# Queries, keys and third weights of a fused attention and two-layer MoE kernel: 154 transposes from fp32 to fp32r, with a new written-out order

## The chip, the cores and the metric

The kernel runs on one core of a Trainium2 chip. The metric is the device time of one execution in microseconds (us); three runs of the kernel before gave a median of 740.92 us (740.73 to 741.88). Five engines work from queues of their own, each strictly in its order: TensorE (PE, with its weight loads shown apart as PEld), VectorE (DVE), ScalarE (ACT), GpSimd (POOL), and SyncE (SP), which here only issues DMAs.

## The reference

For 2 batches of 8 heads, each of 768 positions by 64, queries and keys are assigned to one of 16 clusters (the largest product of the normalized row with normalized centroids). Attention is taken within a cluster: pairs of unequal assignment are masked out. Its output (1536 tokens by 512) goes through two dense layers in sequence.

```python
q_assign = np.argmax(np.einsum('bhsd,hcd->bhsc', q_n, c_n), axis=-1)
k_assign = np.argmax(np.einsum('bhsd,hcd->bhsc', k_n, c_n), axis=-1)
mask = q_assign[:, :, :, None] == k_assign[:, :, None, :]
scores = np.where(mask, scale * np.matmul(q, k.transpose(0, 1, 3, 2)), -1000000000.0)
attn = softmax(scores)
x = np.matmul(attn, v)                   # heads joined: 1536 x 512
h = (x @ w1) * (x @ w2) @ w3 @ w_out     # first layer
g = h2 * clip(h2 + 3, 0, 6) / 6          # with h2 = h @ w_in of the second layer
out = g @ w_out2
```

## The kernel before

Everything on PE is computed to nearly fp32 precision with fp32r operands: each operand is split into a high part (an ACT copy rounded to fp32r) and a low part (the rest, a subtraction), and a product takes three matrix multiplications (high by high, high by low, low by high), or two where operands are stacked.

The work has these stages. **Attention** (to about 350 us) goes head by head: load q and k of a head side by side into one tile of 128 partitions by 6 blocks of 128 columns (`load_qk`, L582 to L585), transpose it by PE in two groups of three (`qk_T`, L605 to L608), take high parts on ACT (`qk_hi`) and low parts on DVE (`qk_lo`), move halves by DMA, compute assignments (`assign_mm` on PE, then nine small steps `oh0` to `oh8`, L651 to L677, on DVE and partly POOL, of which the last transposes the codes, `cd`), and copy the codes into the key and query tiles (`codes_C`). The scores of six blocks c follow (`scores`, L737, a large part and a small part, which waits for the exponential before), then the row maximum on DVE (`smax`, L758), the exponential on ACT (`sexp`, L780), transposes of the exponentials on PE (`p_T`, L796), high and low parts and the product with v (`av`, L820).

**Weights** are brought in meanwhile: each block of 128 by 512 passes through `conv_ops` (two ACT copies, a clamp L1008 on POOL or DVE, two bit operations on DVE, L1017 and L1021). The blocks of w3 are then transposed on PE, four 128 by 128 pieces at a time (`w3_T`, L1037 to L1040), split, and multiplied by w_out (`w_mm`, L1068), so that the first layer's last two matrices become one. Then come the products with w1 and w2 (L1144; from 198 us on beside attention), the combined matrix (L1259 and L1396, to about 485 us) and the second layer (L1707 and L1751) to the end. From the combined matrix on the kernel uses sums of blocks in place of some products, and those sums are DVE's work.

**The order** is written out by hand in a table, `RANK`: each operation of each kind has its place in one sequence of some 4000, and each engine issues its operations in that sequence. A second table, `ON`, says for operations that could run on several engines which one takes it (d, a, p for DVE, ACT, POOL). Room in tile rings is counted when the table is read. `idle_pe` (L529 to L534) puts in 21 multiplications without use, in the first 35 us.

An exponential tile is already transposed as fp32r: `p_raw` (L763 to L772) declares a second tile of type fp32r over the same memory, and writes one padding column of it, so that the transposes have a writer to wait for:

```python
t = at.tile([128, 3 * S + 8], F32R, tag=f"p{hf}", name="praw")
pad = t[:, 3 * S:3 * S + 1]
w = (nc.gpsimd if e == "pool" else nc.vector).tensor_copy(out=pad, in_=three)
...
x = nc.tensor.transpose(pt[:, blk(j)], raw[h, hf][0][:, c, blk(kb)], id_r)
tc.add_manual_dep(x.ins, raw[h, hf][1].ins.name, SYNC)
```

Queries, keys and w3 are transposed as fp32, with the fp32 identity `id_f`.

Of the kernel before, what the change touches and what calls it, by code (L numbers as in the profile page):

```python
# [8 lines left out]
F32 = mybir.dt.float32  # L9
# [73 lines left out]
    "S1": """  # L83
# [3 lines left out]
        1912 1937 1949 1970 1984 2009 2029 2045 2058 2067 2096""",  # L87
    "S": """
# [3 lines left out]
        1892 1925 1940 1960 1979 1994 2015 2034 2049 2069 2088 2101""",  # L92
    "mx": """
# [3 lines left out]
        1899 1928 1944 1968 1982 2000 2019 2038 2053 2073 2090 2107""",  # L97
    "ex": """
# [278 lines left out]
def cluster_attention_moe_kernel(  # L377
# [57 lines left out]
    def blk(i):  # L435
        return slice(i * 128, i * 128 + 128)
# [1422 lines left out]
```

## Time and profile before

| | |
|---|---|
| median of three runs | 740.92 us (740.73 to 741.88) |
| the profiled execution | 741.47 us, its span 739.7 us |
| PE busy | 719.0 us (97%), 4143 instructions |
| PE weight loads busy | 661.4 us (89%) |
| DVE busy | 611.5 us (83%), 1060 instructions |
| ACT busy | 546.8 us (74%), 1043 instructions |
| POOL busy | 201.9 us (27%), 258 instructions |
| DMA moved | 101.97 MB, mean 138 GB/s |

The profile is of one execution. Busy time is what an engine spent in instructions; a matrix multiplication is pipelined, so that the next starts before it ends, and its duration is longer than the step from one to the next. How long an engine needs for one is read from starts. The span runs from the first to the last instruction; the execution's own time lies 1.8 us around it.

### The profile page before, as it was taken

How to read it: one execution, taken by the hardware profiler on the slowest of the kernel's cores; microseconds unless marked ns; L12 is line 12 of the kernel's file. 1: busy time of each engine (PE TensorE's matmuls, PEld its weight loads, DVE VectorE, ACT ScalarE, POOL GpSimd, SP SyncE). 2: the span in 40 equal slices, each digit the busy share in tenths (PEclk: the TensorE clock that was granted, in tenths of full speed). 3: DMA queues.
4: the chain of work that ended last, by engine and by line, in shares of the span. 5: the costliest groups of instructions: out<-in, count | busy, mean ns of one | idle time of the engine just before them, and what ended most of it. 6: DMA issues, size and time to landing. Idle time of an engine off the chain costs nothing. (4 is left out here: it accounts for less than half of the span.)

```text
span 739.7 us, 12102 instructions
## 1 busy us (share of the span) xinstructions
PE 719.0 (97%) x4143; PEld 661.4 (89%) x4143; DVE 611.5 (83%) x1060; ACT 546.8 (74%) x1043; POOL 201.9 (27%) x258
## 2 busy tenths in 40 slices
PE   5699999999999999999999999999999999999998
PEld 4488888888999999999999999999888998998986
DVE  6999999999899888778999999888897666666542
ACT  4899999898888878789867676676666656564543
POOL 3452646332635263355301110110110210011100
PEclk9999999999999999999999999999999999999999
DMA  8668555465563656453566752633222221411202
GB/s 237 157 167 221 152 150 162 114 161 140 150 185 119 182 155 170 115 156 114 178 200 228 238 175 100 220 122 138 91 86 85 72 72 60 137 61 58 72 28 86
DMA packets 81742, 101.97 MB, mean 138 GB/s; under 512 B 30960, under 2 KB 56592, under 8 KB 81680
## 3 DMA queue, kind: packets, MB, share of 16 engines
q1 hardware_dynamic: 81680, 101.20, 45.7%
q8 instruction: 33, 0.54, 0.3%
q14 instruction: 29, 0.24, 0.1%
HBM read 71.34 MB, written 15.78 MB: 118 GB/s over the span
## 5 line engine op out<-in xcount | busy, mean ns | idle before, releaser
L424 DVE TENSOR_TENSOR pl<-ptr,ph 128x512 fp32r<-128x512 f32 x144 | 96.3, 681 | 7.3 <-ACT ph L427 6.9
L758 DVE TENSOR_REDUCE den<-pst 128x1 f32<-128x768 f32 x96 | 91.1, 949 | 10.3 <-PE pst L746 9.2
L427 ACT ACTIVATE ph<-ptr 128x512 fp32r<-128x512 f32 x144 | 84.4, 597 | 14.0 <-PE ptr L796 9.7
L780 ACT ACTIVATE p<-pst,den 128x768 f32<-128x768 f32 x96 | 86.8, 904 | 8.8 <-DVE den L758 7.5
L1144 PE MATMUL psab<-xT,abhl 128*128 128x384 f32 x384 | 81.2, 343 | 0.6 <-DVE g L1154 0.6
L1008 POOL TENSOR_SCALAR cvt<-cvt 128x512 f32<-128x512 f32 x55 | 39.3, 718 | 142.0 <-ACT cvt L427 110.3
L746 PE MATMUL pst<-kk,qkL 128*128 128x512 f32 (+1 forms) x192 | 71.4, 374 | 4.8 <-ACT p L780 4.7
L1144 PEld LDWEIGHTS psab<-xT,abhl 128*128 128x128 f32 x384 | 65.4, 188 | 2.0 <-DVE g L1154 0.9
L820 PE MATMUL av<-ph,vs 128*128 128x384 f32 x192 | 66.4, 346 | 0.0
L796 PEld LDWEIGHTS ptr<-id_r,praw 128*128 128x128 f32 x576 | 60.9, 140 | 5.8 <-DVE pl L424 0.2
L746 PE MATMUL pst<-kk,qkH 128*128 128x512 f32 (+1 forms) x192 | 64.2, 338 | 1.7 <-ACT qkH L427 1.3
L820 PE MATMUL av<-pl,vs 128*128 128x384 f32 x192 | 64.8, 338 | 0.0
L427 ACT ACTIVATE m_sn<-psh 128x384 f32<-128x384 f32 x64 | 31.3, 489 | 44.3 <-PE psh L1707 43.4
L796 PE MATMUL ptr<-id_r,praw 128*128 128x128 f32 x576 | 63.6, 240 | 0.0
L427 ACT ACTIVATE cvt<-raw 128x512 f32<-128x512 f32 x72 | 48.1, 672 | 11.8 <-DVE cvs L1021 6.8
L1017 DVE SCALAR_TENSOR_TENSOR cvs<-cvt,cvs 128x512 int32<-128x512 int32 x72 | 50.0, 696 | 7.5 <-POOL cvt L1008 4.2
L1021 DVE SCALAR_TENSOR_TENSOR cvs<-cvt,cvs 128x512 int32<-128x512 int32 x72 | 50.8, 709 | 0.4
L427 ACT ACTIVATE cvs<-raw 128x512 int32<-128x512 uint8 x72 | 48.1, 670 | 1.8 <-DMA set<-cvs 1.8
L1068 PE MATMUL psw<-woh,wT 128*128 128x512 f32 x128 | 49.3, 405 | 0.0
L746 PEld LDWEIGHTS pst<-kk,qkL 128*128 128x128 f32 x192 | 36.0, 187 | 12.2 <-ACT p L780 9.9
L1751 PE MATMUL po<-m_whl,m_gv 128*128 128x512 f32 x162 | 44.0, 393 | 0.0
L1729 ACT ACTIVATE tt<-m_sn,three 128x384 f32<-128x384 f32 x48 | 29.4, 613 | 18.8 <-DVE m_sn L1717 9.0
(198 smaller groups left out, 1836.0 us busy)
## 6 DMA issues: line engine op xcount, KB each, us to landing
raw<-in_moe_w_dram SPq DMA_DIRECT2D x32, 512.0 KB, 4.3
m_gb<-set SPq DMA_DIRECT2D x64, 256.0 KB, 2.9
raw<-in_moe_w_out_dram SPq DMA_DIRECT2D x24, 512.0 KB, 3.4
raw<-in_moe_w_in_dram SPq DMA_DIRECT2D x16, 512.0 KB, 4.9
set<-cvs SPq DMA_DIRECT2D x32, 256.0 KB, 3.0
kk<-qkH SPq DMA_DIRECT2D x16, 384.0 KB, 4.0
abp<-cvs SPq DMA_DIRECT2D x16, 256.0 KB, 2.8
b_gv<-abp SPq DMA_DIRECT2D x16, 256.0 KB, 4.7
```

The costliest lines, as they stand in the source:

```text
L424: nc.vector.tensor_tensor(out=out, in0=a, in1=b, op=ALU.subtract)
L427: nc.scalar.activation(out=out, in_=in_, func=AF.Copy, **kw)
L746: x = mm(out=psr[:, t, ks_], lhsT=TT[nm, h][:, i, cs_], rhs=flat(TT["K", h][:, a])[:, ks_], start=st, stop=sp)
L758: done["mx", n] = [other_banks(nc.vector.tensor_reduce(out=den_at(h, 0, c), in_=psS[h, c], axis=AX.X, op=ALU.max, negate=True), ("S", n + 1))]
L780: done["ex", n] = [other_banks(nc.scalar.activation(out=p, in_=psS.pop((h, c)), func=AF.Exp, bias=den_at(h, 0, c), accum_out=den_at(h, 1, ...
L796: x = nc.tensor.transpose(pt[:, blk(j)], raw[h, hf][0][:, c, blk(kb)], id_r)
L820: mm(out=t[:, 0:HF], lhsT=vs_t[h][:, 2 * s + i, :], rhs=x_[:, c0:c0 + HF], start=(s == 0 and i == 0 and n == 0), stop=(s == 2 and i == 1 a ...
L1017: stt(out=s, in0=cvt[key], scalar=3, in1=s, op0=ALU.logical_shift_left, op1=ALU.bitwise_or)
L1021: stt(out=s, in0=cvt.pop(key), scalar=-0x80000000, in1=s, op0=ALU.bitwise_and, op1=ALU.bitwise_or)
L1068: mm(out=ps, lhsT=wT[m, hf][:, a, blk(kk)], rhs=w_[hf][:, kk, :], start=(kk == 0 and n == 0), stop=(kk == 3 and n == 2))
L1144: mm(out=ps[:, 0:HF], lhsT=s[:, w, a, blk(kk)], rhs=xT0[0][:, x_, kk, hf * HF:hf * HF + HF], start=(kk == 0 and n == 0), stop=(kk == KD - ...
L1751: mm(out=outs[b, c], lhsT=g[:, a, blk(c % 3)], rhs=w[:, w_, :], start=(first and a == 0 and w_ == 0), stop=(last and a == 1))
```

## The change

Queries and keys of heads 1 to 15 and all blocks of w3 are transposed as fp32r, from a second tile over the same memory, with the fp32r identity `id_r`. For each tile there is a new operation that writes one padding column: `tw` (15 times) and `ww` (16 times), on an engine that `ON` names. Head 0 stays fp32. So that the second tile has the same place as the first, the rings of two and three buffers (`qkn`, `cvs`) become tiles named one by one. The table of places is new throughout, and so is `ON`: seven more clamps stand on DVE (24 for 17), and five more of the one-hot steps `oh1` and `oh4` (8 for 3). The first table lines, and the core of the code:

```diff
-    "lq": "0 1 62 156 297 185 446 611 849 970 1052 1221 1163 1322 1545 1618",
-    "lk": "5 8 96 191 345 403 496 754 886 999 1115 1260 1185 1368 1567 1752",
+    "lq": "0 5 66 131 164 380 458 577 724 900 975 1194 1220 1357 1502 1641",
+    "lk": "4 7 71 212 374 423 466 609 824 956 1008 1208 1380 1462 1611 1676",
...
+    "tw": "ddpappppaaaapaa",
+    "ww": "dpadaadpppaadppp",
...
+    def pad_write(e, pad):
+        if e == "act":
+            return nc.scalar.activation(out=pad, in_=three, func=AF.Copy)
+        return (nc.gpsimd if e == "pool" else nc.vector).tensor_copy(out=pad, in_=three)
...
+    def qk_raw(e, h):
+        del q_n[h]
+        x = ar.tile([128, S + 8], F32R, tag=f"qkn{h % 2}", name="qkr")
+        qraw[h] = x[:, 0:S].rearrange("p (c d) -> p c d", c=NC), pad_write(e, x[:, S:S + 1])
+
     def qk_T(h, hf):
+        if h:
+            x, w = qraw.pop(h) if hf else qraw[h]
+            pt = ps_s.tile([128, HF], F32R, tag="s", name="ptqk")
+            W_["st", h, hf] = pt.bitcast(F32)
+            for c in range(3):
+                i = nc.tensor.transpose(pt[:, blk(c)], x[:, 3 * hf + c, :], id_r)
+                tc.add_manual_dep(i.ins, w.ins.name, SYNC)
+            return
...
+    def w3_raw(e, m, hf):
+        del cvo["w3", m, hf]
+        x = base.tile([128, 520], F32R, tag=f"cvs{held['w3', m, hf]}", name="cvr")
+        wraw[m, hf] = x, pad_write(e, x[:, 512:513])
+
     def w3_T(m, hf):
-        pt = W_["pt", m, hf] = ps_s.tile([128, 4, 128], F32, tag="s", name="pt")
+        x, w = wraw.pop((m, hf))
+        pt = ps_s.tile([128, 4, 128], F32R, tag="s", name="pt")
+        W_["pt", m, hf] = pt.bitcast(F32)
         for i in range(4):
-            nc.tensor.transpose(pt[:, i, :], cvo["w3", m, hf][:, blk(i)], id_f)
-        cvo.pop(("w3", m, hf))
+            j = nc.tensor.transpose(pt[:, i, :], x[:, blk(i)], id_r)
+            tc.add_manual_dep(j.ins, w.ins.name, SYNC)
+        give("w3", m, hf)
```

What the new table moves is shown at three places, all in the first 25 us. The first is SP, at the head of its queue, where the loads of q and k of heads 0 and 1 (`qkn`), the centroids (`cen`), the first block of w3 (`raw`) and v (`vn`) are issued. Before:

```order
L585 DMA qkn<-in_q_dram 128x6x64 x2
L517 DMA cen<-in_centroids_dram 128x64
L989 DMA raw<-in_moe_w_dram 128x1024
L585 DMA qkn<-in_k_dram 128x6x64
L590 DMA vn<-in_v_dram 128x384
```

And now:

```order
L594 DMA qkn<-in_q_dram 128x6x64
L521 DMA cen<-in_centroids_dram 128x64
L1017 DMA raw<-in_moe_w_dram 128x1024
L594 DMA qkn<-in_k_dram 128x6x64
L594 DMA qkn<-in_q_dram 128x6x64
L594 DMA qkn<-in_k_dram 128x6x64
```

The query of head 1 went from the second place to the fifth, so that the centroids, the first w3 block and the key of head 0 each stand one DMA earlier; the key of head 1 went ahead of v.

The second place is DVE, from the first step of head 0's assignment (STREAM_TRANSPOSE from `pa`) to the transposed codes (`cd`); `qkL` is head 1's low part, `cvs` and `cvt` are weight conversions. Before:

```order
L661 STREAM_TRANSPOSE as_239<-pa 128x384
L663 TENSOR_TENSOR as_240<-as_239 128x192
L665 TENSOR_REDUCE as_241<-as_240 128x12
L667 TENSOR_TENSOR as_240<-as_240,as_241 128x192
L618 SCALAR_TENSOR_TENSOR qkL<-ptqk,qks,qkH 128x384
L669 TENSOR_TENSOR as_240<-as_240,wtab 128x192
L1017 SCALAR_TENSOR_TENSOR cvs<-cvt,cvs 128x512
L665 TENSOR_REDUCE as_241<-as_240 128x12
L671 TENSOR_TENSOR ohs<-as_240,as_241 128x12x16
L661 STREAM_TRANSPOSE as_290<-pa 128x384
L677 STREAM_TRANSPOSE cd<-ohs 128x384
```

And now (L1040 is the clamp, L588 a padding column):

```order
L687 STREAM_TRANSPOSE as_242<-pa 128x384
L689 TENSOR_TENSOR as_243<-as_242 128x192
L691 TENSOR_REDUCE as_244<-as_243 128x12
L693 TENSOR_TENSOR as_243<-as_243,as_244 128x192
L695 TENSOR_TENSOR as_243<-as_243,wtab 128x192
L691 TENSOR_REDUCE as_244<-as_243 128x12
L1040 TENSOR_SCALAR cvt<-cvt 128x512
L697 TENSOR_TENSOR ohs<-as_243,as_244 128x12x16
L1040 TENSOR_SCALAR cvt<-cvt 128x512
L644 SCALAR_TENSOR_TENSOR qkL<-ptqk,qks,qkH 128x384
L588 CAST cvr<-three 128x1
L703 STREAM_TRANSPOSE cd<-ohs 128x384
```

Head 1's own first step (`as_290<-pa`) and a conversion no longer stand ahead of `cd`; two clamps and a padding column do.

The third place is ACT, around the first exponential (`p,den<-pst,den`); ACT_TABLE_LOAD and `warm` make the exponential's table ready, `kk<-cd` and `qkH<-cd` copy head 0's codes. Before:

```order
L427 ACTIVATE kk<-cd 16x384
L427 ACTIVATE qkH<-cd 16x384 x2
L427 ACTIVATE cvt<-raw_183 128x512
L506 ACT_TABLE_LOAD
L506 ACTIVATE warm<-three 128x1
L427 ACTIVATE cvs<-raw_183 128x512
L780 ACTIVATE p,den<-pst,den 128x768
```

And now:

```order
L510 ACT_TABLE_LOAD
L510 ACTIVATE warm<-three 128x1
L431 ACTIVATE cvs<-raw 128x512
L431 ACTIVATE kk<-cd 16x384 x2
L431 ACTIVATE qkH<-cd 16x384
L431 ACTIVATE wT<-pt 128x512
L431 ACTIVATE qkH<-cd 16x384
L431 ACTIVATE cvt<-raw_183 128x512
L431 ACTIVATE cvs<-raw_183 128x512
L808 ACTIVATE p,den<-pst,den 128x768
```

The table load moved ahead of the code copies, and both key copies now stand on ACT (one was DVE's).

## Rows read from the trace of the kernel before

**Rows 1.** Busy time by stretch: stretch, length, PE, PEld, DVE, ACT, POOL (instructions), clock, DMA share, GB/s

```profile
40.00:60.00 20.00, 20.00 (x131) 17.90 (x130) 18.90 (x33) 18.34 (x38) 8.76 (x15) 1.00 0.71 182
340.00:360.00 20.00, 19.39 (x123) 18.82 (x123) 17.48 (x28) 17.18 (x30) 10.10 (x7) 1.00 0.54 164
360.00:400.00 40.00, 40.00 (x233) 40.00 (x232) 39.75 (x66) 29.68 (x52) 4.80 (x4) 1.00 0.62 202
400.00:450.00 50.00, 49.79 (x285) 48.97 (x284) 48.40 (x95) 35.59 (x68) 5.92 (x7) 1.00 0.62 202
```

**Rows 2.** Waits of PE from 40 to 736 us: us in total, times, longest

```profile
PE psab L1144 <- DVE g L1154: 0.6, 1, 0.6
PE pst L746 <- DMA qkH<-cd: 0.4, 1, 0.4
PE pst L746 <- ACT p L780: 0.3, 1, 0.3
PE psab L1396 <- DVE b_L L424: 0.2, 1, 0.2
```

**Rows 3.** PE in order of time, around four fp32r transposes: start us, us, instruction

```profile
39.19 0.46 PE L796 MATMUL ptr<-id_r,praw 128*128 128x128 f32 x4
...
39.79 0.39 PE L746 MATMUL pst<-kk,qkH 128*128 128x512 f32 x1
40.02 0.46 PE L796 MATMUL ptr<-id_r,praw 128*128 128x128 f32 x4
```

**Rows 4.** The same around four fp32 transposes

```profile
70.13 0.60 PE L1040 MATMUL pt<-id_f,cvs 128*128 128x128 f32 x4
...
70.69 0.28 PE L746 MATMUL pst<-kk,qkH 128*128 128x256 f32 x1
70.81 0.39 PE L1068 MATMUL psw<-woh,wT 128*128 128x512 f32 x1
```

**Rows 5.** Groups by line, shapes apart: count, busy us, mean ns, idle before

```profile
L796 PE MATMUL ptr<-id_r,praw 128*128 128x128 f32 x576 | 63.6, 240 | 0.0
L1040 PE MATMUL pt<-id_f,cvs 128*128 128x128 f32 x64 | 10.1, 283 | 0.0
```

**Rows 6.** The lines that write padding columns, and the clamp: count, ns min/median/max

```profile
L769 ACT ACTIVATE praw<-three x9: 187/203/218, 111.1 to 300.6; 128x1 fp32r<-128x1 f32 x9
L771 DVE CAST praw<-three x9: 111/154/154, 30.1 to 341.9; 128x1 fp32r<-128x1 f32 x9
L1008 DVE TENSOR_SCALAR cvt<-cvt x17: 412/421/2071, 68.4 to 541.4; 128x512 f32<-128x512 f32 x17
```

**Rows 7.** Start of the program in order of time, SP

```profile
0.74 1.37 SPq L585 DMA_DIRECT2D qkn<-in_q_dram  x2
3.30 0.55 SPq L585 DMA_DIRECT2D qkn<-in_k_dram  x1
```

**Rows 8.** Loads of q and k: from issue to landing

```profile
DMA to landing us min/median/max: 3.0/3.3/6.0
```

**Rows 9.** Start of the program in order of time, PE, DVE and ACT

```profile
7.96 1.52 PE L608 MATMUL ptqk<-id_f,qkn 128*128 128x128 f32 x6 [7.96 <-DMA qkn<-in_k_dram]
11.65 0.66 PE L647 MATMUL pa<-qkH,cT 128*128 128x384 f32 x1 [1.02 <-DVE cT L562]
13.31 0.58 DVE L661 STREAM_TRANSPOSE as<-pa 128x384 f32<-128x384 f32 x1 [0.43 <-PE pa L647]
13.56 2.06 PE L534 MATMUL idle<-id_r 128*128 128x512 f32 x4
15.91 0.68 DVE L1017 SCALAR_TENSOR_TENSOR cvs<-cvt,cvs 128x512 int32<-128x512 int32 x1
18.16 0.58 DVE L661 STREAM_TRANSPOSE as<-pa 128x384 f32<-128x384 f32 x1 [0.92 <-PE pa L647]
18.67 0.54 DVE L677 STREAM_TRANSPOSE cd<-ohs 128x384 f32<-128x384 f32 x1
21.55 0.95 DVE L758 TENSOR_REDUCE den<-pst 128x1 f32<-128x768 f32 x1
21.81 1.28 ACT L506 ACT_TABLE_LOAD   x1
23.76 0.89 ACT L780 ACTIVATE p<-pst,den 128x768 f32<-128x768 f32 x1
```

More of the change, by code (lines that the diff above doesn't have):

```diff
@@ new lines @@
+        2515 2794 2802 2702 3211 2492 2888 2931 3071 2690 2322 3019 2530 3244 2589 2913 2845""",
[6 rows of a table added]
+    "w": """
+        119 160 209 235 257 265 274 277 293 309 323 336 352 356 372 378 399 413 429 440 451 470 489 493 509 532 540 547 569 606 645
+        655 684 704 708 722 766 772 785 813 830 835 846 848 904 914 921 953 980 996 1003 1041 1063 1073 1085 1099 1134 1143 1151 1170
+        1201 1205 1209 1223""",
[6 rows of a table added]
+    "ab": """
[5 rows of a table added]
+        2236 2239 2243""",
+    "aba": "1285 1346 1481 1455 1586 1632 1750 1807 1862 1921 2011 2062 1975 2199 2123 2232",
@@ L215 @@
+    "abg": "1312 1400 1526 1547 1670 1716 1780 1834 1887 1952 2035 2099 2177 2214 2156 2299",
+    "xdone": "2246",
+    "Wh": "2138 2157 2170 2194",
+    "Wl": "2143 2166 2182 2207",
+    "top": "2233",
+    "gsh": "2237 2241 2245 2251 2265 2284 2267 2313",
+    "gsl": "2242 2249 2253 2257 2282 2294 2329 2342",
+    "x2": """
[5 rows of a table added]
+        2947 2950 2952""",
[6 rows of a table added]
     "bsm": """
-        2243 2283 2298 2315 2355 2367 2378 2390 2401 2412 2420 2422 2455 2457 2460 2461 2513 2530 2531 2537 2577 2581 2600 2618 2620
@@ L217 @@
[L217 to L219 removed]
+        2268 2279 2303 2319 2392 2394 2400 2408 2436 2443 2447 2470 2485 2490 2500 2528 2540 2548 2556 2561 2602 2617 2634 2636 2656
+        2658 2674 2682 2708 2713 2725 2740""",
@@ L237 @@
+    "bs": """
+        2381 2397 2405 2411 2439 2453 2462 2467 2493 2512 2517 2523 2550 2575 2588 2596 2613 2627 2631 2637 2657 2669 2675 2681 2699
+        2711 2717 2722 2744 2757 2762 2767""",
[8 rows of a table added]
     "sst": """
-        2532 2403 2328 2132 2105 2257 2349 2379 2269 2428 2199 2598 2559 2451 2196 2491 2853 2818 2707 3120 2482 2888 2931 3147 2705
-        2288 3031 2514 3218 2621 3226 2797""",
+        2549 2418 2344 2025 2174 2347 2389 2401 2281 2451 2220 2695 2607 2471 2278 2520 2797 2829 2748 3215 2497 2949 2936 3246 2693
+        2326 3063 2534 3313 2593 2918 2849""",
@@ L310 @@
+    "oc2": "3560 3568 3584 3599 3573 3621 4017 4015 4032 4018 4028 4026",
+    "os2": "3563 3793 3789 3787 3589 3670 4019 4023 4033 4021 4030 4029",
 }
 ON = {
-    "Ck": "ad",
+    "Ck": "aa",
     "Cq": "aa",
-    "pw": "dppdppppaaapppppapdaddpaadaadpdd",
-    "oh1": "pppppppdppppppp",
-    "oh4": "ppppppppppppppp",
-    "xh": "apaa",
-    "c1": "ppppddpppppppppdppppppppppppppddpppppppppddpppddppppddpdpppppdppppdpdpdd",
-    "woh": "appppppp",
-    "Wl": "ppdd",
+    "pw": "dppdddapdadppppappappdpppddddpad",
@@ L322 @@
+    "tw": "ddpappppaaaapaa",
+    "oh1": "dppppppppppppdd",
+    "oh4": "pppppppppdpddpp",
+    "xh": "appp",
+    "c1": "dppppppppdppppdppppppppppppddppppdpdppppppddpdddpdppdpddppdppddddpdpppdd",
+    "woh": "aapppppp",
+    "ww": "dpadaadpppaadppp",
+    "Wl": "pddp",
     "gsl": "dddddddd",
@@ L325 @@
     "g1s": "dddd",
-    "Ll": "dddddddddpdddddddpdddddpddpdddpd",
-    "wol2": "dddpdpddddddddppdpddddddpdddddpd",
-    "xwl": "dddddddddddddp",
-    "xs": "dpddpddp",
+    "Ll": "dddddddddpddddppdddddddddpddpddd",
+    "wol2": "ddddddddddddddpddppdddddddpddpdp",
+    "xwl": "pdddddddddpddd",
+    "xs": "ddddddpd",
 }
@@ L608, in qk_T @@
             nc.tensor.transpose(pt[:, blk(c)], q_n[h][:, 3 * hf + c, :], id_f)
+        if hf:
+            del q_n[h]
     def qk_hi(h, hf):
@@ L687, in prep_ops @@
         SB = {"p": 0.96, "d": 0.47}
-        op(("lq", h), "dma", 0.7, lambda: load_qk(q, 0, h), due=b - 12, lat=2.0, take=("qn",))
+        op(("lq", h), "dma", 0.7, lambda: load_qk(q, 0, h), due=b - 12, lat=2.0, take=("qn",), after=[("T", h - 2, 1)] * (h > 1))
         op(("lk", h), "dma", 0.7, lambda: load_qk(k, 1, h), [("lq", h)], due=b - 11.9, lat=2.0)
@@ L692, in prep_ops @@
         fop("s", ("vlo", h), SB if h >= WHOLE else {"p": 0.3}, lambda e: v_lo(e, h), (("vhi", h),), due=b - 1.9, drop=("vn",))
+        if h:
+            fop("tw", ("tw", h), {"a": 0.25, "p": 0.12, "d": 0.08}, lambda e: qk_raw(e, h), [("lq", h), ("lk", h)], due=b - 7, lock=False)
         for hf in range(2):
             dd = b - 6.5 + 0.4 * hf
-            op(("T", h, hf), "pe", 0.22, lambda hf=hf: qk_T(h, hf), [("lq", h), ("lk", h)], due=dd, take=("s",),
-               drop=("qn",) if hf else (), after=[("T", h, 0)] * hf)
+            op(("T", h, hf), "pe", 0.22, lambda hf=hf: qk_T(h, hf), [("tw", h)] if h else [("lq", h), ("lk", h)], due=dd, take=("s",),
+               drop=("qn",) if hf else (), after=[("T",) + divmod(2 * h + hf - 1, 2)] * (h + hf > 0))
             op(("qkh", h, hf), "act", 0.375, lambda hf=hf: qk_hi(h, hf), [("T", h, hf)] + [("qkh", h, 0)] * hf, due=dd + 0.05,
@@ L992, in cluster_attention_moe_kernel, with give @@
     ts, stt = nc.vector.tensor_scalar, nc.vector.scalar_tensor_tensor
+    slots, held = list(range(3)), {}
+    def give(*key):
+        slots.append(held.pop(key))
     def conv_ops(key, src, k_, due, big=None):
@@ L1011, in c_low @@
         def c_low(e):
-            s = cvo[key] = base.tile([128, 512], I32, tag="cvs", name="cvs", bufs=3)
+            held[key] = slots.pop(0)
+            s = cvo[key] = base.tile([128, 520], I32, tag=f"cvs{held[key]}", name="cvs")[:, 0:512]
             copy_act(s, raws.pop(key).bitcast(U8)[:, :, 3], scale=1.0 / 32.0, bias=-15.5 / 32.0)
@@ L1060, in wo_lo @@
         sub_on(e, wol[g // 4][:, g % 4, :], cvo.pop(("wo", g)), woh[g // 4][:, g % 4, :])
+        give("wo", g)
     def w_mm(m, g):
@@ L1130, in ab_lo @@
         sub_on(e, abs_[j][:, w, 1], cvo.pop(("ab", j, w)), abs_[j][:, w, 0])
+        give("ab", j, w)
     def ab_store(j, w):
@@ L1592, in set_store @@
         nc.sync.dma_start(out=set_dram[j][:, w], in_=cvo.pop(("set", j, w)))
+        give("set", j, w)
     for j in range(J2):
@@ L1756, in out_copy @@
     def out_copy(b, c):
-        t = W_["osb", b, c] = base.tile([128, DM], F32, tag=("cvt", "cvs")[c % 2], name="osb", bufs=(2, 3)[c % 2])
+        t = W_["osb", b, c] = base.tile([128, DM], F32, tag=f"cvs{(3 * b + c // 2) % 3}" if c % 2 else "cvt", name="osb", bufs=2 - c % 2)
         copy_act(t, outs[b, c], scale=1.0 / 6.0)
```

182 lines of the change are left out of this document (83 added, 99 removed), and 248 rows, old and new, of the table RANK.

## The prediction

> **What bounds the kernel.** I read the busy time by stretch first, then PE's waits, then PE in order of time where the two kinds of transposes stand, then the start. By stretch, PE is busy 20.00 of 20 us at 40 us and 89.79 of 90 from 360 to 450 [rows 1]. A busy PE alone could mean slow matrix multiplications that overlap, so the second view decides: from 40 to 736 us PE waits for another engine in four places, 1.5 us together [rows 2]. There PE sets the pace, and what it is spared comes off the end as long as nobody else becomes late. DVE is close behind: 18.90 of 20 us at 40, and 88.15 of 90 us from 360 to 450 [rows 1]. The first 35 us are another matter: PE waits 7.96 us for the first key, then again for DVE, and DVE and ACT carry a chain to the first exponential [rows 9].
>
> **The transposes.** The step of a group is read from starts, since durations overlap. Four fp32r transposes start at 39.19, and the second multiplication behind them at 39.79; take off the 0.23 that the first of these needs by itself (39.79 to 40.02, one of the same width), and 0.37 us are left [rows 3]. Four fp32 ones: 70.13 to 70.69, less 0.12 (70.69 to 70.81, again the same width), 0.44 us [rows 4]. That is 0.0925 against 0.11 us for one, a saving of 0.0175. The change turns 90 transposes of queries and keys and 64 of w3, 154 in all, 2.70 us. Eight of w3 and twelve of heads 1 and 2 come in the first 34 us, where PE is not what is late; the other 134 give **2.35 us**. Bounds: nothing, if another engine sets the pace as soon as PE is spared, and 134 times the 43 ns by which the mean durations differ (283 and 240) [rows 5], 5.8 us, if the pipeline hid nothing. I stay with the steps, since they are the time that PE's queue really moves on.
>
> The Trainium skill, "TensorE: Matmul & The Clock Gate", Part 4, has a transpose of 128 by 128 take about 275 ns within a kernel, most of it access latency; by that the format would change nothing and this term would be zero. The rows differ from it, 283 ns against 240 and steps of 0.11 against 0.0925 [rows 3 to 5], so I count the rows.
>
> **The padding columns.** There are 31 new instructions: 6 on DVE, 12 on ACT and 13 on POOL. On DVE one takes 154 ns, on ACT 203 [rows 6]; POOL's I take at no more than ACT's. That is 0.9, 2.4 and at most 2.6 us, spread over 16 heads, beside PE, on engines with some idle time (DVE 1.1 us in the 20 us at 40, ACT 1.7 [rows 1]), so I cost them at nothing. What they do add is a second wait: the transposes now hang on an engine's queue, not only on a DMA or on DVE's last bit operation. Nearest to it are the 32 columns that the exponentials already have: no transpose is among the waiting instructions [rows 2]. Bounds: zero, and 31 times the 0.3 us that PE waited for ACT once [rows 2], 9 us. I take zero, since the 32 are the same thing. If the cover went, the next late thing would be head h+1's queries and keys, and with them its scores.
>
> **DVE's load.** The order has seven more clamps on DVE (0.42 each [rows 6], 2.9 us), nine more padding columns (six new, three of the exponentials, 1.4 us), and five one-hot steps, none longer than the 0.58 of a stream transposition [rows 9], 2.9 at most: up to 7.2 us. Its idle time before 340 us takes it (17.48 busy of 20 even at 340 to 360 [rows 1]), if it comes there. I cost it at nothing and price the opposite below.
>
> **The start.** One query load less stands ahead: two issues took 1.37 us [rows 7], so centroids, first w3 block and first key are issued 0.69 us sooner, the key at 2.6 instead of 3.30, and 192 KB less go ahead of it. PE's first transpose goes from 7.96 to 7.27. Head 1's query and key are now issued fifth and sixth, the key near 3.9; with the longest landing of such a load, 6.0 us [rows 8], it is there at 9.9 at the latest, and DVE's first padding column, which waits for it between two low parts, stands near 9.4: a delay of 0 to 0.5 us, and I take none, as 3.3 is the median.
>
> What the first 0.69 us bring is partly lost at once: four idle multiplications now stand ahead of the first assignment product on PE, 2.06 us where they stood [rows 9]. Before, PE waited 1.02 us there. With its release 0.69 sooner (10.96) and about 1.0 of the idle block outside the gap, the product starts between 10.96 and 12.0 (before 11.65); I take 11.8, 0.15 late.
>
> On DVE the stretch from there to the codes was 5.36 us (13.31 to 18.67). A wait of 0.92 us, head 1's first step (0.58) and a conversion (0.68) no longer lie in it [rows 9], two clamps (0.84) do: 1.3 us shorter at most. With the 0.15 the codes come 1.1 us sooner. Between them and the first maximum the order now has one more conversion, head 1's first two steps and one code copy less, 0.68 + 0.58 + 0.36 - 0.47 = 1.15 us if all run back to back (the last two are my estimates for half of a 0.68 conversion and for a copy of codes), so that the maximum stays at 21.55 and ends at 22.50. But the first exponential, which came at 23.76 behind the table load (21.81) and a copy, finds the table ready: it can start at 22.50, **1.26 us sooner** [rows 9]. Each of the next exponentials follows from the one before by the small part of the scores and a maximum, so this shift goes on to where PE becomes full. Bounds: nothing, if ACT's extra copies or the weight loads hold this loop, and 1.26 + 0.69 = 1.95 if the 0.69 isn't lost either. I take **1.0 us**, between them.
>
> **The sum.** The profiled execution took 741.47 us, 0.55 more than the median of the runs. Less 2.35 and 1.0 it is 738.1; beside the median **737.6 us**. A measurement of this kernel can tell about 0.2%, 1.5 us, from no change: faster means under 739.4, slower over 742.4.
>
> **The rivals.**
>
> *The start brings nothing.* The DMA's 192 KB or the idle block eat the 0.69, and conversions hold the first exponentials. For it: ACT has a second code copy and a second high part of w_out in this stretch. Against: the table load is off the chain in any case. 740.92 - 2.35 = 738.6 us. Chance 0.13.
>
> *The new waits take back what the transposes save.* A padding column behind a 0.9 us exponential on ACT or a long POOL subtraction makes PE wait 0.1 us at each of 31 places, 3 us, all of the gain: 740.9 us. Against it: 32 such columns with no wait in rows 2. Chance 0.11.
>
> *The format saves nothing*, so the change does not do on PE what it says: the step is set by loading weights and by access, as wide in both formats. Then only the start counts, 740.92 - 1.0 = 739.9 us. Against it are the two steps of rows 3 and 4. Chance 0.05. The Trainium skill's page named above would have it this way.
>
> *DVE becomes the bound, and the kernel slower.* From 360 to 450 us DVE has 1.85 us idle [rows 1], and PE's sums of blocks wait for it there. It decides from the point where more than 1.85 of DVE's 7.2 new us fall into this stretch. If all did, 738.1 + 7.2 - 1.85 = 743.5, and 742.9 beside the median. Against it: from the last maximum to the ninth sum with a product the order holds nine clamps for seven, but one low part, one conversion and one sum fewer. For it, a sentence of its own: the Trainium skill, "SBUF — State Buffer", "Who interferes with whom", says that copies and scalar operations of DVE may take a port that it shares with GpSimd and that either then waits for the other's whole instruction. One of 17 clamps here did take 2071 ns for 421 [rows 6], the others did not. Chance 0.11.
>
> *The start gives all it can and more.* The start gains 1.95 us, and the steps shrink by half of the difference to what the mean durations would give: 740.92 - 1.95 - 2.35 is 736.6, and with another 1.7 us, half of 5.8 less 2.35, it is 734.9. Chance 0.08.
>
> That leaves 0.52 for the forecast. Faster than 739.4 are nearly all of it (0.49), most of the first rival (0.11) and the last (0.08): 0.68. Within 0.2% are the third, most of the second and the edges: 0.19. Slower: 0.13, the fourth rival and the upper end of the second. The range leaves out the far ends of the last and the fourth: 734.8 to 741.6 us.
>
> **What would show it.** In the changed kernel's profile the fp32r groups of w3 (`cvr`) and queries (`qkr`) should have the step of 0.37 us for four and durations near 240 ns, and PE's first transpose should start near 7.3. The first exponential should start near 22.5. PE's waits from 40 us on should stay near 1.5 us with no `ptqk` or `pt` among them; if these appear, the padding columns are late. DVE should show idle time from 360 to 450; if PE's combined-matrix products (`psab`) wait for DVE by more than a microsecond there, the fourth rival holds. The forecast is wrong if PE's own steps are unchanged, or if the sum of PE's waits grows by the 2.35 us that it is spared.

## The result, and the profile after

The changed kernel takes 750.07 us (747.60 to 752.07, 6 runs) where the kernel before takes 741.45 beside it: a ratio of 1.0112, 95% interval 1.0088 to 1.0135. It is slower by 8.3 us (6.5 to 10.0). The forecast was 737.6 and its range ended at 741.6. The profiled execution took 747.82 us with a span of 746.0, so it lies near the fast end of the runs, and its trace can show 6.3 of the 8.3 us (747.82 less 741.47).

The busy times of the changed kernel, from its page:

```profile
PE 722.7 (97%) x4143; PEld 662.1 (89%) x4143; DVE 617.2 (83%) x1082; ACT 546.9 (73%) x1051; POOL 196.3 (26%) x259
```

What answers to [rows 2], PE's waits from 40 to 745 us (us in total, times, longest):

```profile
PE po L1798 <- DVE m_hl L428: 2.9, 1, 2.9
PE av L848 <- DVE pl L428: 1.8, 1, 1.8
PE psh L1754 <- DVE m_sn L1764: 0.9, 1, 0.9
PE psab L1442 <- ACT b_sn L431: 0.2, 1, 0.2
```

5.8 us in place of 1.5, and 5.6 of it for DVE. None of these waits is for a transpose or a padding column.

The loss lies behind 340 us. The last of the 96 row maxima on DVE starts 2.0 us sooner than in the kernel before, 337.5 for 339.5 us (before, then changed; the last number of the times is the start of the last maximum):

```profile
L758 DVE TENSOR_REDUCE den<-pst x2: 936/942/948, 336.4 to 339.5; 128x1 f32<-128x768 f32 x2
...
L786 DVE TENSOR_REDUCE den<-pst x1: 949/949/949, 337.5 to 337.5; 128x1 f32<-128x768 f32 x1
```

The first product with the up weights (`psx`) starts 0.7 us sooner (358.2 for 358.9), the first of the second layer (`psh`) 1.2 later (486.1 for 484.9), and the last of all 6.1 later (741.7 for 735.6). Where the largest wait comes from stands in DVE's and POOL's order of time around 555 and 575 us (start us, us, instruction):

```profile
552.09 0.95 DVE L428 TENSOR_TENSOR x2f<-x2f 128x768 f32<-128x768 f32 x1
...
554.84 2.40 DVE L1661 TENSOR_TENSOR m_gb<-m_gb 128x256 f32<-128x256 f32 x2
...
572.85 0.42 DVE L1661 TENSOR_TENSOR m_gb<-m_gb 128x256 f32<-128x256 f32 x1
573.19 3.70 DVE L428 TENSOR_TENSOR x2f<-x2f 128x768 f32<-128x768 f32 x1
576.81 1.74 DVE L428 TENSOR_TENSOR m_hl<-m_gb,m_hl 128x512 fp32r<-128x512 f32 x1
...
555.07 1.89 POOL L425 TENSOR_TENSOR x2f<-x2f 128x768 f32<-128x768 f32 x1 [21.50 <-DVE m_gA L428]
572.91 3.15 POOL L425 TENSOR_TENSOR m_gB<-m_gb,m_gB 128x1280 fp32r<-128x1280 f32 x1 [15.95 <-ACT m_gB L431]
576.03 1.98 POOL L425 TENSOR_TENSOR m_w<-m_gb,m_w 128x512 fp32r<-128x512 f32 x1
```

The same block sum on DVE, `x2f` of 128x768, took 0.95 us at 552.09. Begun 0.28 us after a POOL subtraction of 3.15 us it took 3.70 and ended at 576.89, 0.83 after POOL's end at 576.06: nearly all of its own work came behind POOL's. The next step took 1.74 in the same way beside the next POOL step. The chain of waits runs through these two. At 347 us the picture is the same, and PE's wait of 1.8 us follows from it for the most part (run 10, without this POOL step, keeps 0.8):

```profile
347.21 3.50 DVE L1050 SCALAR_TENSOR_TENSOR cvs<-cvt,cvs 128x512 int32<-128x512 int32 x2
...
347.54 2.61 POOL L425 TENSOR_TENSOR Whl<-W,Whl 128x1024 fp32r<-128x1024 f32 x1 [1.42 <-ACT Whl L431]
```

Two of these bit operations take 1.3 us otherwise. The table `ON` had put the four POOL steps there: a pair of low parts, a block sum, and the low part of the up weights.

The kernel before has such pairs too. Here a DVE step that takes 0.55 us otherwise is put off to the end of a POOL step (POOL's, then DVE's):

```profile
665.16 3.22 POOL L421 TENSOR_TENSOR m_gB<-m_gb,m_gB 128x1280 fp32r<-128x1280 f32 x1 [4.59 <-ACT m_gB L427]
665.77 3.02 DVE L1733 SCALAR_TENSOR_TENSOR tt<-tt,m_sn 128x384 f32<-128x384 f32 x1 [0.22 <-ACT tt L1729]
```

PE does not wait behind it [rows 2]. A pair shows as a loss where PE waits for its DVE step.

The start, which answers to [rows 9], PE, DVE and ACT in order of time:

```profile
7.14 1.51 PE L632 MATMUL ptqk<-id_f,qkn 128*128 128x128 f32 x6 [7.14 <-DMA qkn<-in_k_dram]
...
11.66 0.52 PE L673 MATMUL pa<-qkH,cT 128*128 128x384 f32 x1
...
16.12 0.44 PE L673 MATMUL pa<-qkH,cT 128*128 128x384 f32 x1 [0.97 <-ACT qkH L641]
17.24 0.51 PE L673 MATMUL pa<-qkL,cT 128*128 128x384 f32 x1 [0.67 <-DVE cvr L588]
...
20.38 0.79 PE L774 MATMUL pst<-kk,qkH 128*128 128x512 f32 x1 [1.45 <-ACT qkH L431]
...
22.69 0.88 ACT L808 ACTIVATE p<-pst,den 128x768 f32<-128x768 f32 x1
```

The first transpose comes 0.8 us sooner and the first exponential 1.07. But a product of 512 columns takes 0.79 us at 20.38; 0.39 is usual [rows 3], and behind a pause of 1.30 us it took 0.50 in the kernel before. The reason stands in the stretches (PE busy is the second number, the granted clock the third from the end):

```profile
15.00:18.00 3.00, 1.36 (x7) 0.91 (x6) 2.97 (x9) 2.97 (x5) 0.38 (x1) 0.91 0.52 139
18.00:21.00 3.00, 1.55 (x5) 0.84 (x5) 2.53 (x5) 2.89 (x7) 0.18 (x1) 0.50 0.98 335
...
24.00:27.00 3.00, 2.94 (x8) 1.93 (x8) 2.87 (x6) 2.62 (x6) 2.32 (x3) 0.50 1.14 188
27.00:30.00 3.00, 3.00 (x12) 2.14 (x11) 2.07 (x4) 2.06 (x4) 0.82 (x2) 0.88 1.01 192
```

PE paused for 0.97 and 0.67 us between 15.1 and 17.3 us, and from about 17.5 to 27.7 us it had a granted clock of 0.50, the lower of its two levels (1.2 GHz); the pause of 1.45 us came when the clock had already fallen. The idle products that stood ahead of the first scores in the kernel before had moved behind the second group.

The format did what the prediction said of it on PE. Read as the prediction reads them, four transposes of w3 take 0.38 us (median of 14 groups), where the kernel before takes 0.44. In place of 283 ns [rows 5] they now show (count, busy, mean ns):

```profile
L627 PE MATMUL ptqk<-id_r,qkr 128*128 128x128 f32 x90 | 11.0, 244 | 0.8 <-DVE qkr L588 0.5 <-DVE pl L428 0.3
...
L1082 PE MATMUL pt<-id_r,cvr 128*128 128x128 f32 x64 | 8.0, 252 | 0.0
```

### The profile page after: what moved, and what is told of

Same layout as the page of the kernel before. It is cut to its first block, busy times and chain, and to the rows that moved or that the text cites. A ratio compares the mean times of both kernels' runs of the same rounds, so it can differ in the third digit from the quotient of the medians.

```text
span 746.0 us, 12119 instructions
## 1 busy us (share of the span) xinstructions
PE 722.7 (97%) x4143; PEld 662.1 (89%) x4143; DVE 617.2 (83%) x1082; ACT 546.9 (73%) x1051; POOL 196.3 (26%) x259
## 4 chain that ended last, share of the span: by engine, by line
PE 53%; DVE 6%; ACT 2%; issue 2%; POOL 0%; DVEq 0%; ACTq 0%
PE po L1798 16%; PE psh L1754 14%; PE psab L1442 7%; PE psx L1305 6%; PE psab L1190 4%; PE av L848 2%; PE pst L774 2%; PE ptr L824 1%; DVE x2f L428 1%; DVE m_gb L1661 1%; DVE cvs L1050 0%; DVE cvs L1054 0%; DVE m_hl L428 0%; ACT cvt L431 0%; DVE m_gv L428 0%
## 5 line engine op out<-in xcount | busy, mean ns | idle before, releaser
L1040 POOL TENSOR_SCALAR cvt<-cvt 128x512 f32<-128x512 f32 x48 | 35.0, 732 | 129.7 <-ACT cvt L431 73.3
L1112 PE MATMUL psw<-woh,wT 128*128 128x512 f32 x128 | 50.8, 409 | 0.0
L1798 PE MATMUL po<-m_hl,m_gv 128*128 128x512 f32 x144 | 39.5, 394 | 2.9 <-DVE m_hl L428 2.9
```

The lines of the kernel that those rows point to most:

```text
L1798: mm(out=outs[b, c], lhsT=g[:, a, blk(c % 3)], rhs=w[:, w_, :], start=(first and a == 0 and w_ == 0), stop=(last and a == 1))
```

## The experiments

Of the two theories the first was: **A**, the format saves what its steps save, and the new order loses some 11 us. The rival **B**: the second tiles and their padding columns cost by themselves. After the twelfth run a third came in, **C**, the tiles' places in memory. "Over" and "under" below are against the kernel before on the same chip, the ratio less one times 741.4.

| run | median us | over (+) or under (-) the kernel before, interval |
|---|---|---|
| changed kernel | 750.07 | +8.3 (6.5 to 10.0) |
| 1 old order, format | 765.03 | +22.8 (21.1 to 24.5) |
| 2 new order, no format | 749.22 | +7.5 (6.5 to 8.5) |
| 3 changed, second part old | 743.93 | +2.2 (1.2 to 3.3) |
| 4 run 1, second part new | 766.94 | +25.4 (24.3 to 26.3) |
| 5 old order, columns on DVE | 743.76 | +2.2 (1.4 to 3.1) |
| 6 changed, more idle products | 749.31 | +8.1 (6.7 to 9.4) |
| 7 changed, two low parts on DVE | 747.65 | +6.0 (4.7 to 7.4) |
| 8 runs 3 and 6 together | 742.99 | +1.6 (0.8 to 2.4) |
| 9 as 5, columns mostly on POOL | 742.83 | +1.9 (1.1 to 2.5) |
| 10 changed, mended | 743.50 | +2.4 (1.4 to 3.4) |
| 11 before, keys sooner | 740.64 | -0.6 (-1.3 to +0.1) |
| 12 before, 31 DVE columns more | 742.84 | +2.0 (1.3 to 2.8) |
| 13 before, 32 bytes more | 742.25 | +0.9 (0.2 to 1.5) |
| 14 run 9, 64 bytes | 741.44 | +0.1 (-0.5 to +0.8) |
| 15 run 10, 64 bytes | 742.43 | +1.0 (0.4 to 1.7) |
| 16 run 14, keys sooner | 740.67 | -0.7 (-1.5 to +0.1) |
| 17 run 16, 128 bytes | 743.04 | +1.3 (0.4 to 2.3) |
| 18 run 10, 128 bytes | 742.79 | +2.1 (1.1 to 3.0) |

**Order and format apart (1 to 4).** Run 1 keeps `RANK` and `ON` of before and puts the new operations in, as far ahead of their transposes as the new table has them; the two memory slots of `qkn` are handed out in turn, since the old order loads a head out of turn. Run 2 has the new tables without the new operations. Runs 3 and 4 change from one table to the other at `top`, where the second part opens its tiles.

```diff
-        x = ar.tile([128, S + 8], F32R, tag=f"qkn{h % 2}", name="qkr")
+        x = ar.tile([128, S + 8], F32R, tag=f"qkn{qs[h]}", name="qkr")
```

> The order of the kernel before, with the fp32r transposes and their second tiles put in (each padding column as many places ahead of its transposes as in the changed kernel). Theory A (the loss comes from the new order, the format saves what its steps save): 738.5 to 739.5 us, since 134 transposes that count give back 2.35 us and nothing else moves; TensorE's granted clock stays at 1.00 from 18 us on. Theory B (the second tiles themselves cost: the padding columns in the queues of VectorE, GpSimd and ScalarE, and the waits of TensorE on them): 744 us or more, with TensorE waiting for qkr and cvr.

> The order of the changed kernel without the padding columns, and the fp32 transposes of the kernel before. Theory A: as slow as the changed kernel and slower by the 2.35 us that the format gave, 750 to 753 us, with the long waits of the changed kernel (the second layer's product waiting for VectorE near 576 us) still there. Theory B: 741 to 743 us, since the second tiles are gone.

> The changed kernel up to the point where the second part begins (about 345 us), and from there the order and the choice of engines of the kernel before. Theory A: the changed kernel stood 0.7 us ahead at 358 us and lost 6.8 us behind it, so about 740.7 us (739.5 to 742), and no wait of TensorE over 1 us behind 400 us. Theory B, or a loss that follows from the phase in which the first part ends: 746 us or more.

> The first part in the order of the kernel before with the fp32r transposes (as in the first run), and the second part in the order of the changed kernel. Theory A: 1.7 to 2.4 us ahead at 358 us, then the 6.8 us that the second part lost in the changed kernel: 745 to 747 us, with the granted clock at 1.00 from 18 us on. If the loss behind 540 us comes from the way in which the first part ends, 739 us.

Run 2 is nearly as slow as the changed kernel and has its waits of 2.9 and 1.8 us: the loss is the order's. Run 3 takes 6.1 us of it away with the second part alone, near the 6.8 that A had put behind 358 us; its 743.93 us still miss A's range of 739.5 to 742. But run 2 was to be 2.35 us slower than the changed kernel and wasn't, and run 1 missed by 26 us. Its trace says why (130 to 225 us, all engines' waits):

```profile
POOL qkr L576 <- DMA qkn<-in_k_dram: 9.7, 2, 5.2
...
ACT qkr L575 <- DMA qkn<-in_k_dram: 8.4, 2, 4.6
```

The old order loads a head just in time. A padding column waits for the load, and where it stands in POOL's or ACT's queue some places ahead, everything behind it waits too. Behind these waits the clock fell too (0.83 from 170 to 210 us), and a part of the loss is the clock's. So run 1 measured my placing; and run 4, which shares its first part, is 2.6 us above run 1 where 6.8 were expected, with the same wait of 2.9 us in it, and tells little more.

**The format in the old order (5 and 9).** Run 5 puts each column on DVE, after what it waits for has surely come; run 9 puts 23 of them on POOL in the same manner.

```diff
-    "tw": "ddpappppaaaapaa",
+    "tw": "ddddddddddddddd",
-    "ww": "dpadaadpppaadppp",
+    "ww": "dddddddddddddddd",
```

> The order before with the fp32r transposes, as in the first run, but every padding column on VectorE: a third weight's directly behind the sign step of its conversion, a head's directly ahead of the VectorE step that began 0.8 to 1.5 us before its transposes in the kernel before, so long after its queries and keys have landed. Theory A (the format saves what its steps save; the 23.5 us that the first run lost came from padding columns that stood in the queues of GpSimd and ScalarE ahead of the landing of their head's keys): 738.5 to 739.5 us, no wait of TensorE over 1 us between 130 and 225 us. Rival (second tiles cost by themselves): over 743 us.

> The order before with the fp32r transposes as in the fifth run, but 23 of the 31 padding columns on GpSimd, at places where it stood idle or between steps after what they wait for had come, and the other 8 on VectorE. If VectorE's load between 50 and 200 us (39.4 of 40 us busy at 120 to 160) ate the format's 2.35 us in the fifth run: 740 to 742 us, 2 us under it. If TensorE's waits for a padding column cost, whatever engine writes it: 743 to 744 us again.

The 20 us of run 1 are gone, so its cause was the queues. But no saving is left in either run: 2.2 and 1.9 us over, where theory A wanted 2.35 under.

**The start and the late waits (6, 7, 8 and 10).** Run 6 raises one group of idle products from four to eight and moves another from place 103 to 70, ahead of the first scores. Run 7 changes two letters of `Ll`, run 10 these, one of `xs` and one of `Wl`, with the products of run 6. Run 8 is run 3 with run 6's products.

```diff
-    "Ll": "dddddddddpddddppdddddddddpddpddd",
+    "Ll": "dddddddddpdddddddddddddddpddpddd",
```

> The changed kernel, with filler products put back into TensorE's pauses ahead of the first scores: the three that stood behind the second score group go back ahead of the first, and the four behind the first head's assignment become eight. If the half clock of 17 to 27 us (granted 0.50) follows from the pauses at 15 to 20 us: granted clock 1.00 from 12 us on, the first softmax steps up to 2 us sooner, 746.5 to 748.5 us. If the clock falls all the same, or the first stage is set by ScalarE and VectorE anyway: 749.5 to 751 us.

> The changed kernel, with one pair of low parts of the second layer (those of 128x1280 and 128x512 that GpSimd computed at 572.91 and 576.03 us) on VectorE, as in the kernel before. If TensorE's wait of 2.9 us at 576 us comes from VectorE's step of 3.70 us beside GpSimd's 3.15 us: that VectorE step takes about 0.95 us, the wait goes, and the time falls by 2 to 3 us, to 747 to 748 us. If VectorE is simply too full there: the wait stays, 749.5 to 751 us.

> The changed kernel's first part with the filler products of the second run of this call, and the second part in the order of the kernel before. If both causes add up: 1 to 2 us less than the run with the second part alone in the old order (743.9 us), so 741.5 to 743 us, and the spread of its runs under 2 us. If the clock at the start costs nothing, 743.9 us again.

> The changed kernel with the filler products of the sixth run, and with four GpSimd steps on VectorE that stood beside a stretched VectorE step: the pair of low parts at 572.91 and 576.03 us, the block sum at 555.07 and the low part of the up weights at 347.54. If each stretched VectorE step is the price of the GpSimd step beside it: TensorE's waits at 350 us (1.8) and 576 us (2.9) go, and the time is 744 to 746 us, 4 to 5 us under the changed kernel. If only the pair matters: 747 us.

In run 7 the two DVE steps are back to their usual time, and PE's wait at 576 us is gone:

```profile
575.79 0.95 DVE L416 TENSOR_TENSOR x2f<-x2f 128x768 f32<-128x768 f32 x1
576.65 0.69 DVE L416 TENSOR_TENSOR m_hl<-m_gb,m_hl 128x512 fp32r<-128x512 f32 x1
```

That is 2.3 us by the ratios (0.1 to 4.5, from the two intervals). Run 10 is 5.9 us faster than the changed kernel, and 5.7 (4.0 to 7.4) faster than run 6, from which it differs by the four letters alone. Its waits from 40 us on are

```profile
PE av L836 <- DVE pl L416: 0.8, 1, 0.8
PE psh L1742 <- DVE m_sn L1752: 0.3, 1, 0.3
```

The DVE steps beside POOL's were thus the largest part of the loss. The clock of the start was not: run 6 held it at 1.00 up to 24 us, but then it fell all the same, behind a stretch with PE busy for 1.15 of 3 us,

```profile
21.00:24.00 3.00, 1.15 (x6) 0.91 (x6) 3.00 (x6) 2.90 (x7) 1.63 (x3) 1.00 1.13 263
24.00:27.00 3.00, 1.79 (x7) 1.31 (x6) 2.73 (x6) 2.90 (x6) 2.15 (x3) 0.65 1.02 192
```

and the gain, 0.2 us by the ratios and 0.8 by the medians, is not told from nothing. In the traces the 24th row maximum starts at 96.9 to 98.1 us with run 6's products (runs 6, 8, 10, 15, 18) and at 97.5 to 98.2 without (changed kernel, runs 3 and 7). DVE was busy for all 3.00 us there and ACT for 2.90, so they seem to hold the start. Run 8 stands 0.6 us under run 3, which is not told from nothing either.

Two losses of the new order stand in some of its profiles and not in others. At 103 to 105 us ACT waits 0.2 to 1.3 us for a block of w_out in runs 2, 3, 6 and 7 (here run 7),

```profile
ACT cvt L419 <- DMA raw<-in_moe_w_out_dram: 1.3, 1, 1.3
```

and from the 24th to the 36th row maximum these four take 39.0 to 39.9 us, the changed kernel and runs 8, 10, 15 and 18, without this wait, 37.8 or 37.9. And behind PE's wait of 1.8 us near 352 us the clock fell for 3.4 us in runs 7 (here) and 8, but not in the changed kernel and runs 3 and 6:

```profile
354.00:357.00 3.00, 2.90 (x10) 2.91 (x11) 1.70 (x4) 0.48 (x1) 0.51 (x1) 0.57 0.14 57
```

From the last row maximum to the first up product runs 7 and 8 take 22.2 or 22.3 us, the other three 20.6 or 20.7. The changed kernel's own profile has neither loss, and is 2.2 us under its median. Whether the two make up these 2.2 us no run shows; they do blur what runs 6 to 10 say of each other. The changed kernel's profile and run 10's, neither with these losses, differ by 5.1 us (747.82 and 742.68), near the 5.7.

**The keys alone (11).** In the kernel before three loads move back, and what stood between them moves up a place.

```diff
-    "lq": "0 1 62 156 297 185 446 611 849 970 1052 1221 1163 1322 1545 1618",
+    "lq": "0 5 62 156 297 185 446 611 849 970 1052 1221 1163 1322 1545 1618",
-    "lk": "5 8 96 191 345 403 496 754 886 999 1115 1260 1185 1368 1567 1752",
+    "lk": "4 7 96 191 345 403 496 754 886 999 1115 1260 1185 1368 1567 1752",
-    "lv": "6 159 204 284 490 729 592 859 1059 1188 1102 1538 1310 1669 1734 1962",
+    "lv": "8 159 204 284 490 729 592 859 1059 1188 1102 1538 1310 1669 1734 1962",
```

> The kernel before with two queue places alone changed: the second head's queries and the first head's values behind the first head's keys. The prediction's term for the start: first transposes at 7.2 instead of 7.96 us, first softmax step up to 1 us sooner, 740.4 us. If the start is set by what stands behind the transposes (ScalarE and VectorE up to 22 us): 741.4 us, no change.

First transpose and first exponential in its trace:

```profile
7.25 1.51 PE L596 MATMUL ptqk<-id_f,qkn 128*128 128x128 f32 x6 [7.25 <-DMA qkn<-in_k_dram]
...
23.12 0.89 ACT L768 ACTIVATE p<-pst,den 128x768 f32<-128x768 f32 x1
```

0.71 and 0.64 us sooner than [rows 9], and 0.6 us in the time. It is as expected, though the interval just reaches no change. Other profiles bear it out: with the sooner keys in the old order (runs 11, 16, 17) the first transposes start at 6.95 to 7.25 us and the first exponentials at 22.50 to 23.12; without (kernel before, runs 1, 4, 5, 9, 12, 13, 14) at 7.89 to 8.42 and at 23.02 to 24.49.

**Columns without format, and the tiles' places (12 to 18).** Run 12 writes the 31 columns of run 5 to a scratch tile and leaves the fp32 transposes. Run 13 only declares that tile, 32 bytes in each partition. Runs 14, 15 and 16 make the padding 16 columns in place of 8, runs 17 and 18 make it 32; 16 and 17 have the sooner keys too.

```diff
+    pad = const.tile([128, 8], F32R, name="pad")
...
-        x = base.tile([128, 520], F32R, tag=f"cvs{held['w3', m, hf]}", name="cvr")
+        x = base.tile([128, 528], F32R, tag=f"cvs{held['w3', m, hf]}", name="cvr")
```

> The kernel before, fp32 transposes and all, with 31 VectorE columns more: each at the place of a padding column of the fifth run, written to a scratch tile that nobody reads. If VectorE's added steps cost the time that the fifth run lost (it stood 2.3 us over the kernel before, 4.7 over what the format should have given): 743 to 746 us, more than the fifth run. If a full VectorE hides behind TensorE: 741.4 us, and the fifth run's loss comes from the fp32r transposes or their waits.

> The kernel before with one tile of 32 bytes per partition more, which nothing writes or reads: the tiles that stand behind it in memory move from 32 to 0 modulo 64, the up weights and the keys' tiles do not. Theory C (a product whose two operands stand at unlike addresses modulo 64 steps slower): the up products of the shared part (up weights and gated tile) step at 175 ns or more in place of 173, and the time is 742.3 to 743.0 us, as with the 31 added columns. Rival (the added columns themselves cost): 741.2 us, no change.

> The ninth run (old order, fp32r transposes, padding columns mostly on GpSimd) with 16 columns of padding in place of 8, so that every tile moves by multiples of 64 bytes and the residues are those of the kernel before. Theory C: the up products step at 173 ns again and the time falls to 739.5 to 741 us, 2 us under the ninth run, so that a part of the format's saving shows. Rival: 742.8 us, as the ninth run.

> The tenth run (the changed kernel with filler products and four GpSimd steps moved) with 16 columns of padding in place of 8. Theory C: 741 to 742.3 us, 1.2 to 2.5 us under the tenth run (743.5). Rival: 743.5 us.

> The fourteenth run with the sooner keys of the eleventh: theory C and the 0.6 us of the eleventh run add up: 739 to 740.4 us, under both kernels. If the sooner keys need the old padding or order: as the fourteenth run.

> The sixteenth run with 32 columns of padding in place of 16 (128 bytes). If operands at equal addresses modulo 128 are what the up products want: their median step falls from 338 to 334 ns, and the time by 384 x 2 ns and more, to 739.5 to 740.3 us, clearly under the kernel before. If not: 740.7 us and 338 ns.

> The fifteenth run (changed order, mended) with 32 columns of padding in place of 16. If 128 is what counts: up products at 334 ns, 741.2 to 742.0 us. If not: 742.4 us and 338 ns.

Run 13 does no work that the kernel before doesn't, and its up products take longer. The kernel before, run 13 and run 14 (ns min/median/max):

```profile
L1259 PE MATMUL psx<-gh,Whl x192: 333/334/335, 358.9 to 421.5; 128*128 128x384 f32 x192
```

```profile
L1261 PE MATMUL psx<-gh,Whl x192: 334/340/342, 359.2 to 422.1; 128*128 128x384 f32 x192
```

```profile
L1297 PE MATMUL psx<-gh,Whl x192: 331/338/339, 358.0 to 420.8; 128*128 128x384 f32 x192
```

The weights `Whl` lie at byte 196576 of a partition in all three programs; the gated tile moves from 133344 to 133376 and 133536. Run 13 costs 0.9 us (0.2 to 1.5), and the 31 DVE columns then 1.1 us more (run 12; 0.1 to 2.1). Padding of 64 bytes gives 1.8 us back in the old order (run 14 against 9; 0.8 to 2.8) and 1.4 in the new (15 against 10; 0.2 to 2.6), near what C expected. But the up products did not return to 334, so what I named as C's carrier is not it: in run 13's trace the whole stretch from the first up product to the first product of the second layer is only 0.2 us longer (126.2 for 126.0). With 128 bytes the gain is lost again (run 17 is 2.0 us over run 16, run 18 1.1 over run 15; 337 ns). Run 16 just missed its range, and run 17 fits neither of its two expectations. That a shift of tiles alone moves this kernel by 1 to 2 us is shown; by which rule is open.

Run 14 also shows where the format's saving went. DVE's row maxima in the kernel before, then in run 14:

```profile
L758 DVE TENSOR_REDUCE den<-pst x1: 957/957/957, 39.5 to 39.5; 128x1 f32<-128x768 f32 x1
...
L758 DVE TENSOR_REDUCE den<-pst x1: 952/952/952, 197.0 to 197.0; 128x1 f32<-128x768 f32 x1
```

```profile
L778 DVE TENSOR_REDUCE den<-pst x1: 959/959/959, 39.6 to 39.6; 128x1 f32<-128x768 f32 x1
...
L778 DVE TENSOR_REDUCE den<-pst x1: 953/953/953, 196.9 to 196.9; 128x1 f32<-128x768 f32 x1
```

The second of these maxima, 48 further on, comes 157.5 us behind the first in the one and 157.3 in the other, though 104 transposes between them (56 of w3, 48 of heads 3 to 10) were shortened, worth 1.8 us by the prediction's steps. PE's busy time from 120 to 160 us shows it from the other side, in the kernel before and in run 14; DVE's, the third number, is the same:

```profile
120.00:160.00 40.00, 39.93 (x259) 35.06 (x258) 39.52 (x68) 35.46 (x74) 17.73 (x27) 1.00 0.54 148
```

```profile
120.00:160.00 40.00, 39.72 (x257) 34.89 (x257) 39.52 (x70) 35.35 (x73) 18.80 (x30) 1.00 0.53 143
```

So DVE, busy for all but 0.48 of the 40 us in both, seems to hold the pace there. That is read from these rows; no run took work off DVE in this stretch to show it. Behind 197 us run 14 does gain: its last row maximum starts at 338.6 us for 339.5.

No version beat the kernel before beyond doubt: runs 11 and 16 stand 0.6 and 0.7 us under it, with intervals that reach +0.1.

## Why the prediction was wrong, step by step

*"DVE's load ... I cost it at nothing."* This step failed most. I counted clamps, columns and one-hot steps, put them against idle time, and gave the fourth rival its place at 360 to 450 us. What cost most was not DVE's own load but four POOL steps that `ON` had set beside DVE's: at 347, 555, 573 and 576 us. Moved to DVE, which loads it further, they give back 5.7 us (run 10 against run 6), and the pair alone 2.3 (run 7). What the clamps and one-hot steps cost by themselves no run shows. The prediction had the mechanism in hand, a clamp of 2071 ns for 421 [rows 6], and asked it only of clamps and of one stretch; the letters of the second layer in `ON` it didn't read at all. The Trainium skill, "SBUF — State Buffer", "Who interferes with whom", says more than I took from it: a VectorE step that reads two tensors from SBUF contends with a GpSimd step that reads SBUF, and what they share is an exclusive lock. The trace agrees: the stretched steps (0.95 to 3.70, two of 1.3 to 3.50) all have both inputs in SBUF, and they ended behind POOL's.

*"There PE sets the pace."* This holds at most from 200 us on, not from 40. A busy PE with 1.5 us of waits in all [rows 2] looked like the bound, with DVE "close behind". In run 14 PE was spared and the row maxima kept the old pace up to 197 us: many waits too small for that view seem to have taken the saving. So **the transposes' 2.35 us** were sized rightly as steps (0.38 us for four) and wrongly as time: run 14, with columns, format and places together, stands 0.1 us over the kernel before (-0.5 to +0.8). The bound at its lower end, "nothing, if another engine sets the pace as soon as PE is spared", was nearer. The Trainium skill, "TensorE: Matmul & The Clock Gate", Part 4, gives one figure for a transpose, some 275 ns within a kernel. The trace agrees with it for fp32 (283 ns [rows 5]) and not for fp32r (244 and 252).

*"The padding columns ... I cost them at nothing."* From 40 us on no transpose of the changed kernel waited for them: of the new PE waits none is theirs. In the start one did, 0.54 us at 9.40 us, for which the prediction had 0 to 0.5 and took none. But 31 of them on DVE cost 1.1 us (run 12 less run 13), and in a queue ahead of a load that hasn't landed they cost 20 (run 1 less run 5). The bound of 9 us was too low for that, and the cover that I named, the exponentials' columns, doesn't wait for a DMA.

*"The start ... 1.0 us."* The size was near: 0.6 us when made alone (run 11), first transpose at 7.25 for the 7.27 forecast. In the changed kernel PE began at 7.14 and the first exponential came at 22.69 for the 22.50 forecast. That it fits so closely is partly luck: with the same tables runs 3 and 7 had it at 21.78 and 22.13. Then the scores ran at the lower clock, and at 40 us the shift was gone (seventh row maximum at 40.2 us for 39.5). I had moved idle products about in the sum and priced them as time in a queue, not as what goes before the clock's fall; run 6 says that this cost little, since DVE and ACT hold that stretch.

*No term at all* stood for the wider tiles. The prediction says that they become tiles named one by one; that 8 columns in each of three tiles move most of the memory by 96 bytes it doesn't say. Shifts like it made 0.9 to 1.8 us (runs 13, 14, 15).

By the ratios the 8.3 us are then: 5.9 for the POOL steps with the idle products (run 10), 1.4 for the tiles' places (run 15 against 10), and 1.0 that is left in run 15, whose cause stays open. The traces show where it lies: from the first up product to the first product of the second layer the new order takes 127.3 to 128.2 us in all eight profiles that have its second part (mended or not, with the format or without), the old one 125.5 to 127.1 in the other twelve. The three numbers are differences along one chain of runs, not shares measured each by itself. Against them stands what the changed kernel had won by its last row maximum, 2.0 us in its profile, of start, format and order together.

## What to carry to other kernels

When a table of places or of engines is replaced, read it for pairs: a GpSimd step and, at the same time, a VectorE step with both inputs in SBUF for which the bottleneck waits; or a queue entry that waits for a DMA ahead of work that doesn't. A bottleneck engine without visible waits may still share the pace with another that is 95 to 99% busy; before a saving on it is counted, look whether the other's own steps would come sooner. And a tile made wider moves its neighbours: compare the time before and after, even where the work is the same. One profile may lack a loss that other executions of the same kernel have: here a late load and a fall of the clock stood in some profiles of one order and not in others.

## What the runs showed that was not expected

An fp32 subtraction of VectorE took 3.70 us in place of 0.95 beside one of GpSimd: not shared, but put off to its end. The clock's fall doesn't follow from a pause's length alone: after pauses of 0.97 and 0.67 us it was granted at 0.50 from 17.5 to 27.7 us, while the kernel before kept 1.00 through pauses of 1.30 and 2.33 us between 19 and 25 us, with PE busy throughout from 12 to 18 us ahead of them; and behind the same wait of 1.8 us near 352 us it fell in runs 7 and 8 and not in the changed kernel. And a product's time can depend on where its operands lie: 334 ns or 337 to 340 for the same 128x384 with the same weights' address, and 1 to 2 us for the whole kernel.
